# An eighth pair by plain products in the first block, and fewer dummy products in the lead, in a block-attention and feed-forward kernel

## The chip, the cores and the metric

The kernel runs on one core of one Trainium2 chip. The metric is the device time of one execution in microseconds (us), less is better. The five engines are named as in the profile: PE (TensorE, matrix products), DVE (VectorE), ACT (ScalarE), POOL (GpSimd) and SP (the engine whose queue issues most DMAs). PSUM is the memory into which PE writes, in eight banks; SBUF is the working memory.

## What is computed

Attention within chunks of 64 tokens, then a feed-forward layer with squared ReLU, all in float32:

```
q, k, v: (8 batches, 8 heads, 576 tokens, 64); 9 chunks of 64 tokens per batch and head
scores = q_c @ k_c.T / 8                 # per chunk and head
attn   = exp(scores - max) / (sum + 1e-9)
x      = (attn @ v_c), heads side by side    # 4608 tokens x 512
out    = (relu(x @ w_in) ** 2) @ w_out       # 512 -> 2048 -> 512
```

The weights `w_in` and `w_out` are float64 and reach the chip as two 32-bit words per element.

## The kernel before

**Pairs, units, blocks.** Two chunks are a pair (128 tokens, 36 pairs). Half of a pair's heads are a unit, so a pair has two. `blocks = [4] + [3] * 10 + [2]` (L63) groups the pairs into twelve blocks of 4, 3 and 2. For each block the feed-forward runs 16 steps (`NF`): step f multiplies x by 128 columns of `w_in` (`mm_in`, L603 to L612), ACT and DVE square the result and split it, and two steps later (`LAG`) `mm_out` (L647 to L656) adds its product with 128 rows of `w_out` to the block's output in PSUM. x, the squares and the weights are each held as a high and a low half in the format fp32r, and three products (high x high, high x low, low x high) stand for one. The last step of a block copies its outputs from PSUM (`store`, L658, copies on L663 and L665) and writes them out.

**Two ways through the attention.** The first `NN` pairs (seven: those of blocks 0 and 1) go by plain float32 products, class `Pair` (L472 to L581): PE turns q and k (L488), ACT copies them to `qbd` and `kt` (L497, L501), 16 score products (L509), DVE takes maximum, difference, sum and scaling (L517 to L535) with ACT's exponential between (L526), PE turns the probabilities (L547), ACT copies them (L552), 16 products with v (L561), and `place` writes x as high (ACT, L579) and low half (DVE, L581). All later pairs go by split halves, which cost PE less and DVE, ACT and POOL more: `s1` to `s4` and `norm` (L284 to L455), for one unit at a time. Their products are spread evenly among the feed-forward's products by `merge` (L682): while block b's steps run, the slots of block b + 1's units run beside them. Slot t holds the scores of unit t-1, the transposes of t-2 and the values of t-3, and so on (`attention_slot`, L585). Block 1 has twelve slots: one that opens the split path's tiles (`open_late`, L103), two empty ones (`HEAD`), and nine with attention (units 14 on, L923 to L927). Later blocks have six.

**The first block.** Block 0 also has to convert all 32 pieces of the weights (items) from float64 to two halves (`convert_w`, L142: two operations of ACT, four of DVE, then the high half on ACT, L182, and the low half on DVE, L191). Its order on all engines is written out by a planner (`Plan`, L697): operations are added with a cost, what they read and write, and a rank; at each step it takes the one that can start earliest, then the lowest rank. SP's operations are kept in the order in which they were added, so a load that waits for its room holds up all loads behind it. First comes the lead: four pairs with q, k and v from HBM, PE being given dummy bf16 products (`heat`, L779, 30 of them, and `warm_up`, L566, eight ahead of scores, turned probabilities and values of each of the four pairs). Pairs 4 to 6 follow among the conversions, added when the item number reaches 8, 14 and 20 (L889).

**Rooms.** Each item has a room of its own, `w0` to `w31`. Raw q and k of pair u lie in room `w31-u` until they are turned (L223), so the fetches of items 25 to 31 wait for that. v of a plain pair lies in `vbd0` or `vbd1`, by `pair % 2` (L99, L261); the load of pair 2's v waits until pair 0's products with v are done. Pairs outside the lead take all five PSUM tiles from the two banks named `at` (L805). x of blocks with even numbers shares one room, of odd ones another (`x_of`, L457).

Of the kernel before, what the change touches and what calls it, by code (L numbers as in the profile page):

```python
# [10 lines left out]
F32 = mybir.dt.float32  # L11
# [9 lines left out]
def kernel(  # L21
# [20 lines left out]
    nc = tc.nc  # L42
# [21 lines left out]
    LAG = 2  # L64
    HEAD = 2
    REST = 0
    GBUFS = 2
    RBUFS = 1

    WARM = 30  # L70
    WARM_P = 8
# [3 lines left out]

    NN = sum(blocks[:2])
    first_pair = [sum(blocks[:b]) for b in range(len(blocks))]
# [21 lines left out]
    qbd = [nat.tile([P, H, 2, CH], F32, name=f"qbd{n}") for n in range(2)]  # L99
    vbd = [nat.tile([P, H // 2, 2, 2, D], F32, name=f"vbd{n}") for n in range(2)]  # L100
    late = {}

    def open_late():  # L103
# [148 lines left out]
    def load_v(pair):  # L252


        if pair < NN:
            for c in range(2):
                bb, n0 = divmod(2 * pair + c, NCH)
                for h2, r in enumerate(halves):
                    s = v[bb, h2:H:2, n0 * CH:(n0 + 1) * CH, :]
                    nc.sync.dma_start(  # L260
                        out=vbd[pair % 2][r, :, c, h2, :], in_=s.rearrange("h i d -> i h d")  # L261
                    )
            return
        pairs[pair]["v"] = []
        for c in range(2):
            t = late["pool"].tile([P, H, D], F32, name=f"v_raw{pair}_{c}", tag="v_raw")
            pairs[pair]["v"].append(t)
            bb, n0 = divmod(2 * pair + c, NCH)
            s = v[bb, :, n0 * CH:(n0 + 1) * CH, :].rearrange("h i d -> i h d")
            for r in halves:  # L270
                nc.sync.dma_start(out=t[r], in_=s)
# [196 lines left out]
    def bank(which, shape, name):  # L468
        kind, n = which
        return psum[kind].tile(shape, F32, name=name, tag=f"{kind}{n}")  # L470

    class Pair:  # L472

# [21 lines left out]
        def keep_q(self, s):  # L495
            r = halves[s]
            nc.scalar.copy(qbd[self.u % 2][r, :, s], self.psq[r])  # L497

# [4 lines left out]
        def scores(self):  # L503


            self.sc = self.bank("sc", [P, H, CH])
            self.warm_up(self.sc.rearrange("p a b -> p (a b)"))
            for h in range(H):
                nc.tensor.matmul(  # L509
                    self.sc[:, h // 4 * 4 + h % 2 * 2 + h // 2 % 2],  # L510
                    qbd[self.u % 2][:, h].rearrange("p s i -> p (s i)"), self.kt[:, h],
                    start=True, stop=True,
                )
# [25 lines left out]
        def turn_p(self):  # L539


            ps = self.bank("pt", [P, HS // 2, 2, 2, CH])
            self.warm_up(ps.rearrange("p a b c d -> p (a b c d)"))
            e = self.e.rearrange("p (a c t) i -> p a c (t i)", t=2, c=2)
            for a in range(HS // 2):
                for c in range(2):
                    nc.tensor.transpose(ps[:, a, c].rearrange("p s i -> p (s i)"), e[:, a, c], ident)  # L547
            self.pt = ps
# [5 lines left out]
        def values(self):  # L554

            self.xt = self.bank("xt", [P, HH, 2, CH])
            self.warm_up(self.xt.rearrange("p a b c -> p (a b c)"))
            for hp in range(HH):
                s, a = divmod(hp, HS // 2)
                for c in range(2):  # L560
                    nc.tensor.matmul(  # L561
                        self.xt[:, hp, c], vbd[self.u % 2][:, hp, c].rearrange("p a d -> p (a d)"),
                        self.t[:, a, c, s], start=True, stop=True,
                    )

        def warm_up(self, ps):  # L566


            if self.lead:
                for _ in range(WARM_P):  # L570
                    nc.tensor.matmul(ps[:, :2 * P], warm_ops[:, :P], warm_ops, start=True, stop=True)

# [9 lines left out]

    warm_ops = ident.bitcast(mybir.dt.bfloat16)

# [11 lines left out]
    class Step:  # L596
# [6 lines left out]
        def mm_in(self, c, i):  # L603
            if c == 0 and i == 0:
                self.h = bank(("h", self.f % 2), [P, DM], f"h{self.b}_{self.f}")
            xh, xl = xt[self.b]
            wh, wl = wi[self.f]
# [160 lines left out]
    def first_block():  # L768


        p = Plan()
        add = p.add
        prs = [Pair(u) for u in range(NN)]

# [12 lines left out]
        def fetch(n):  # L787
            room = [("raw", n), ("q", n_items - 1 - n), ("k", n_items - 1 - n)]
            add(SP, ISSUE, lambda: fetch_w(n), writes=room, size=P * DM * 8)
# [6 lines left out]
        def load_values(u):  # L796
            add(SP, 4 * ISSUE, lambda: load_v(u), writes=[("v", u % 2)], size=P * DM * 4)

        def attention(u):
# [9 lines left out]
            for s in range(2):  # L809
                add(ACT, ONE, lambda s=s: x.keep_q(s), [bq], [("qbd", i, s)])  # L810
            add(PE, 4 * 0.11, lambda: x.turn(1), [("k", u), "ident"], [bk])
            add(ACT, ONE, x.keep_k, [bk], [("kt", i)])
            w = WARM_P * 0.11 if x.lead else 0
            add(PE, 16 * 0.11 + w, x.scores, [("qbd", i, 0), ("qbd", i, 1), ("kt", i)], [bs])
# [6 lines left out]
            add(ACT, ONE, x.keep_p, [bp], ["tt"])  # L821
            add(PE, 16 * 0.11 + w, x.values, [("v", i), "tt"], [bx])
            add(ACT, ONE, lambda: x.place(0), [bx], [("xh", u)])
            add(DVE, TWO, lambda: x.place(1), [bx, ("xh", u)], [("xl", u)])

# [37 lines left out]
        add(PE, WARM * 0.11, heat, ["ident"], [("at", 0)])  # L863
        for t in (qbd[0], vbd[0], qbd[1], vbd[1]):
            add(POOL, 0.95, lambda t=t: zero(t), [], [("qbd", i, s) for i in range(2) for s in range(2) if t is qbd[i]] + [("v", i) for i in range(2) if t is vbd[i]])
        lead = blocks[0]
        load(0)
        load_values(0)
        load(1)
        load_values(1)  # L870
        for u in range(2, lead):
            load(u)
        got = 2
        for n in range(got):
            fetch(n)
        for u in range(lead):
            p.rank = u
            attention(u)
            if u + 2 < lead:
                load_values(u + 2)  # L880
                fetch(got)
                got += 1
        for n in range(got):
# [3 lines left out]
        for n in range(got, n_items):  # L887
            p.rank = NN + n
            if u < NN and n >= 2 * got + 6 * (u - lead):  # L889
                load(u)  # L890
                load_values(u)
                attention(u)
                u += 1
            fetch(n)
            convert(n)
        add(SP, 16 * ISSUE, lambda: load_qk(NN), writes=["late"], size=2 * P * DM * 4)
        for f in range(NF):
# [4 lines left out]
            p.rank = -1  # L902
            square(f)
        p.run()

# [4 lines left out]
    with tc.manual_schedule(engines={PE}):  # L910
        for b in range(1, len(blocks)):
# [10 lines left out]
            if not last:  # L922
                n0 = NQ * first_pair[b + 1]  # L923
                n1 = n0 + NQ * blocks[b + 1]
                slots = [list(attention_slot(t, NQ * NN)) for t in range(n0 + 3 * (b > 1), n1 + 3)]
            if b == 1:
# [39 lines left out]
```

## Time and profile before

| what | us |
|---|---|
| median of 3 runs | 956.59 |
| lowest, highest | 955.41, 956.65 |
| the profiled execution | 956.33 |
| its span, first to last instruction | 954.2 |
| PE, DVE, ACT, POOL busy | 928.7, 708.5, 601.5, 216.8 |

The span is one profiled execution; the time is measured around it. In a line of the profile, `L609 PE MATMUL h<-xh,wi ... x1536 | 435.6, 340 | 3.0 <-DVE wi L191 1.6` is: line of the kernel, engine, operation, what is written from what, how many, busy time in us, mean duration of one in ns, and the engine's idle time ahead of them with what ended most of it. Products on PE are pipelined, so their durations overlap: the pace of PE is read from the distances between starts or from the chain of waits, not from the mean duration. A line of the timeline or of the chain begins with start and duration in us; `x12` means twelve instructions run together. A line of the windows has the stretch, its length, then busy time of PE, PE's weight loads (PEld), DVE, ACT and POOL, the granted TensorE clock as a share, the DMA share and GB/s.

### The profile page before, as it was taken

What the parts mean: (1) busy time and instruction counts of PE and PEld (TensorE: products, weight loads), DVE (VectorE), ACT (ScalarE), POOL (GpSimd) and SP (SyncE); (2) the same over time, 40 slices, a digit from 0 to 9 for tenths busy, and PEclk for the clock granted to TensorE, in tenths of its full rate; (3) what the DMA queues carried; (4) which work ended last, traced back from release to release, by engine and by line L of the source; (5) the groups of instructions that cost most, each with busy time, mean ns of one, the idle gap of its engine ahead of it and who ended that gap; (6) DMA issues with size and microseconds to landing.
All of it is one profiled execution on the core that took longest, in us unless ns stands there. A gap on an engine that the chain in (4) does not pass through costs nothing.

```text
span 954.2 us, 16935 instructions
## 1 busy us (share of the span) xinstructions
PE 928.7 (97%) x5046; PEld 828.8 (87%) x5046; DVE 708.5 (74%) x1634; ACT 601.5 (63%) x1491; POOL 216.8 (23%) x361
## 2 busy tenths in 40 slices
PE   9899999887999999999999999999999999999998
PEld 7788878766999999989999989989999999998997
DVE  3989995888777877777877877877878787753332
ACT  5688874677666766666766766666666666653232
POOL 1000002134222322333333323322222233311000
PEclk9999999999999999999999999999999999999999
DMA  6794505445533543433544544444444353210000
GB/s 161 192 295 136 177 1 117 85 92 105 111 74 75 111 77 71 104 74 74 111 78 78 111 79 75 94 93 78 77 109 81 72 113 62 56 40 9 4 34 23
DMA packets 292761, 86.06 MB, mean 90 GB/s; under 512 B 274112, under 2 KB 282304, under 8 KB 292672
## 3 DMA queue, kind: packets, MB, share of 16 engines
q1 hardware_dynamic: 290560, 84.47, 40.5%
q8 instruction: 41, 0.67, 0.3%
q10 hardware_dynamic: 2112, 0.52, 0.3%
q14 instruction: 48, 0.39, 0.1%
HBM read 52.69 MB, written 9.44 MB: 65 GB/s over the span
## 4 chain that ended last, share of the span: by engine, by line
PE 88%; DVE 5%; ACT 2%; DMA 2%; SPq 1%; issue 1%; POOL 0%; DVEq 0%; ACTq 0%; POOLq 0%
PE h L609 39%; PE o L653 38%; PE sc L346 3%; PE xt L430 3%; PE pt L396 1%; DMA woraw<-in_moe_w_out_dram 1%; PE sc L509 1%; SPq L250 1%; PE warm_ps L782 1%; PE xt L561 1%; ACT kst L305 0%; DMA k_raw<-in_k_dram 0%; DVE wi L191 0%; DVE wia L170 0%; ACT qst L299 0%
## 5 line engine op out<-in xcount | busy, mean ns | idle before, releaser
L609 PE MATMUL h<-xh,wi 128*128 128x384 f32 (+2 forms) x1536 | 435.6, 340 | 3.0 <-DVE wi L191 1.6
L653 PE MATMUL o<-wo,gh 128*128 128x512 f32 x1152 | 372.9, 397 | 0.0
L609 PEld LDWEIGHTS h<-xh,wi 128*128 128x128 f32 x1536 | 275.5, 189 | 18.4 <-DVE wi L191 3.1
L609 PE MATMUL h<-xl,wi 128*128 128x384 f32 (+2 forms) x768 | 261.1, 340 | 1.1 <-DVE xl L581 1.1
L653 PEld LDWEIGHTS o<-wo,gh 128*128 128x128 f32 x1152 | 208.5, 188 | 33.5 <-issue 0.2
L653 PE MATMUL o<-wo,gl 128*128 128x512 f32 x576 | 227.1, 394 | 0.0
L327 POOL TENSOR_TENSOR vs<-v_raw,vs 64x128 fp32r<-64x128 f32 x232 | 119.9, 517 | 250.1 <-ACT vs L324 234.3
L636 DVE TENSOR_TENSOR gl<-g,gh 128x384 fp32r<-128x384 f32 (+2 forms) x192 | 110.9, 578 | 64.5 <-ACT gh L633 60.9
L609 PEld LDWEIGHTS h<-xl,wi 128*128 128x128 f32 x768 | 145.0, 189 | 8.1 <-DVE xl L581 1.4
L624 DVE TENSOR_TENSOR g<-g 128x384 f32<-128x384 f32 (+1 forms) x176 | 99.2, 564 | 67.5 <-ACT g L620 65.7
L633 ACT CAST gh<-g 128x384 fp32r<-128x384 f32 (+2 forms) x192 | 98.5, 513 | 76.4 <-PE o L653 52.9
L620 ACT ACTIVATE g<-h 128x384 f32<-128x384 f32 (+2 forms) x192 | 94.5, 492 | 78.5 <-PE h L609 58.8
L653 PEld LDWEIGHTS o<-wo,gl 128*128 128x128 f32 x576 | 108.5, 188 | 20.5
L383 POOL TENSOR_TENSOR e<-e,z 128x256 f32<-128x256 f32 x58 | 46.0, 793 | 227.0 <-PE o L653 88.7
L358 DVE TENSOR_TENSOR e<-sc,e 64x128 f32<-64x128 f32 x232 | 67.0, 289 | 35.0 <-ACT e L356 30.3
L356 ACT COPY e<-sc 64x128 f32<-64x128 f32 x232 | 60.3, 260 | 47.4 <-PE sc L346 44.5
L444 DVE TENSOR_TENSOR x<-xt,x 64x128 f32<-64x128 f32 x232 | 67.0, 289 | 22.8 <-ACT x L442 17.5
L442 ACT COPY x<-xt 64x128 f32<-64x128 f32 x232 | 60.1, 259 | 35.8 <-PE xt L430 32.2
L346 PE MATMUL sc<-kst,qst 128*128 128x256 f32 x232 | 65.7, 283 | 5.5 <-DVE pst L414 3.3
L430 PE MATMUL xt<-pst,vs 128*128 128x256 f32 x232 | 65.2, 281 | 1.9 <-DMA pst<-pst 1.7
L450 POOL TENSOR_TENSOR xl<-x,xh 128x256 fp32r<-128x256 f32 x58 | 46.0, 793 | 61.0 <-ACT xh L449 58.7
L414 DVE TENSOR_TENSOR pst<-pt,pst 64x256 fp32r<-64x256 f32 x116 | 49.0, 422 | 11.7 <-ACT pst L410 7.7
(78 smaller groups left out, 909.3 us busy)
## 6 DMA issues: line engine op xcount, KB each, us to landing
v_raw<-in_v_dram SPq DMA_DIRECT2D x116, 128.0 KB, 3.3
out_dram<-ob SPq DMA_DIRECT2D x36, 256.0 KB, 2.1
wiraw<-in_moe_w_in_dram SPq DMA_DIRECT2D x16, 512.0 KB, 6.4
woraw<-in_moe_w_out_dram SPq DMA_DIRECT2D x16, 512.0 KB, 6.2
q_raw<-in_q_dram SPq DMA_DIRECT2D x232, 32.0 KB, 2.0
k_raw<-in_k_dram SPq DMA_DIRECT2D x232, 32.0 KB, 2.1
qst<-ql SPq DMA_DIRECT2D x58, 128.0 KB, 2.6
kst<-kst SPq DMA_DIRECT2D x58, 128.0 KB, 2.6
```

Source lines behind the costliest of these rows:

```text
L327: nc.gpsimd.tensor_tensor(vs[:, c][dst], vr[dst], vs.bitcast(F32)[:, c][dst], op=ALU.subtract)
L346: nc.tensor.matmul(ps.rearrange("p w c j -> p (w c j)"), late["q"][:, hh].rearrange("p c i -> p (c i)"), late["k"][:, :, :, hh], start=Tru ...
L356: nc.scalar.copy(e[r], ps[r, :, 1, c])
L358: nc.vector.tensor_tensor(e[r], ps[r, :, 0, c], e[r], op=ALU.add)
L430: nc.tensor.matmul(st["xt"][hp][:, c].rearrange("p w a q -> p (w a q)"), st["v"][:, c, hp].rearrange("p a d -> p (a d)"), late["p"][:, :, ...
L444: nc.vector.tensor_tensor(x[r, hp], ps[hp][r, :, 0, h2], x[r, hp], op=ALU.add)
L609: nc.tensor.matmul(self.h[:, :self.n], a[:, c], bb[:, c, :self.n], start=c == 0 and i == 0, stop=c == NCC - 1 and i == 2,)
L620: nc.scalar.activation(self.g, self.h[:, :self.n], AF.Relu)
L624: nc.vector.tensor_tensor(self.g, self.g, self.g, op=ALU.mult)
L633: nc.scalar.copy(self.gh[:, :self.n], self.g)
L636: nc.vector.tensor_tensor(self.gl[:, :self.n], self.g, self.gh.bitcast(F32)[:, :self.n], op=ALU.subtract)
L653: nc.tensor.matmul(acc[b, j], a[:, j * P:(j + 1) * P], bb, start=f == 0 and i == 0, stop=f == NF - 1 and i == 2,)
```

## The change

Five things change.

- `NN` becomes 8: the first pair of block 2 also goes by plain products, in block 0's stretch. Its x belongs to block 2, whose room is that of block 0's x, so its `place` is added after the last step of block 0. In the order of attention outside the lead, pairs now follow every four items (8, 12, 16, 20). Block 1's slots begin at unit 16: seven instead of nine.
- `HEAD` becomes 1: one empty slot instead of two. Block 1 has nine slots in all.
- Dummy products: 18 instead of 30 at the start; eight ahead of each of three stages for the first and the last pair of the lead only; and eight more ahead of the first product of the feed-forward.
- v of pairs 2 and 3 gets rooms of its own, in `w22` and `w21`, whose items are fetched after these pairs' values. With that the loads of the lead are put in another order: q and k of three pairs ahead of the first v, and the fetches of four items among the rest.
- The second half of q's copy moves from ACT to DVE for pairs 0 and 1.

```diff
--- before.py
+++ after.py
@@ -62,18 +62,19 @@
     PRIO = 300
     blocks = [4] + [3] * 10 + [2]
     LAG = 2
-    HEAD = 2
+    HEAD = 1
     REST = 0
     GBUFS = 2
     RBUFS = 1
 
-    WARM = 30
+    WARM = 18
     WARM_P = 8
     assert sum(blocks) == NPAIR
     MAXB = max(blocks)
     XB = (max(blocks[::2]), max(blocks[1::2]))
 
-    NN = sum(blocks[:2])
+
+    NN = sum(blocks[:2]) + 1
     first_pair = [sum(blocks[:b]) for b in range(len(blocks))]
 
     const = ctx.enter_context(tc.tile_pool(name="const", bufs=1))
@@ -98,7 +99,13 @@
     nat = early.enter_context(tc.tile_pool(name="nat", bufs=1))
     qbd = [nat.tile([P, H, 2, CH], F32, name=f"qbd{n}") for n in range(2)]
     vbd = [nat.tile([P, H // 2, 2, 2, D], F32, name=f"vbd{n}") for n in range(2)]
+
+    for n in range(2, blocks[0]):
+        vbd.append(const.tile([P, H // 2, 2, 2, D], F32, name=f"vbd{n}", tag=f"w{2 * DFF // P - NN - n}"))
     late = {}
+
+    def slot_of(pair):
+        return pair if pair < blocks[0] else pair % 2
 
     def open_late():
 
@@ -258,7 +265,7 @@
                 for h2, r in enumerate(halves):
                     s = v[bb, h2:H:2, n0 * CH:(n0 + 1) * CH, :]
                     nc.sync.dma_start(
-                        out=vbd[pair % 2][r, :, c, h2, :], in_=s.rearrange("h i d -> i h d")
+                        out=vbd[slot_of(pair)][r, :, c, h2, :], in_=s.rearrange("h i d -> i h d")
                     )
             return
         pairs[pair]["v"] = []
@@ -469,6 +476,14 @@
         kind, n = which
         return psum[kind].tile(shape, F32, name=name, tag=f"{kind}{n}")
 
+    warm_ops = ident.bitcast(mybir.dt.bfloat16)
+
+    def warm_up(ps):
+
+
+        for _ in range(WARM_P):
+            nc.tensor.matmul(ps[:, :2 * P], warm_ops[:, :P], warm_ops, start=True, stop=True)
+
     class Pair:
 
 
@@ -494,7 +509,9 @@
 
         def keep_q(self, s):
             r = halves[s]
-            nc.scalar.copy(qbd[self.u % 2][r, :, s], self.psq[r])
+
+            copy = nc.vector.tensor_copy if s and self.u < 2 else nc.scalar.copy
+            copy(qbd[self.u % 2][r, :, s], self.psq[r])
 
         def keep_k(self):
             self.kt = nat.tile([P, H, CH], F32, name=f"kt{self.u}", tag=f"kt{self.u % 2}")
@@ -504,7 +521,8 @@
 
 
             self.sc = self.bank("sc", [P, H, CH])
-            self.warm_up(self.sc.rearrange("p a b -> p (a b)"))
+            if self.u in (0, blocks[0] - 1):
+                warm_up(self.sc.rearrange("p a b -> p (a b)"))
             for h in range(H):
                 nc.tensor.matmul(
                     self.sc[:, h // 4 * 4 + h % 2 * 2 + h // 2 % 2],
@@ -540,7 +558,8 @@
 
 
             ps = self.bank("pt", [P, HS // 2, 2, 2, CH])
-            self.warm_up(ps.rearrange("p a b c d -> p (a b c d)"))
+            if self.u in (0, blocks[0] - 1):
+                warm_up(ps.rearrange("p a b c d -> p (a b c d)"))
             e = self.e.rearrange("p (a c t) i -> p a c (t i)", t=2, c=2)
             for a in range(HS // 2):
                 for c in range(2):
@@ -554,21 +573,15 @@
         def values(self):
 
             self.xt = self.bank("xt", [P, HH, 2, CH])
-            self.warm_up(self.xt.rearrange("p a b c -> p (a b c)"))
+            if self.u in (0, blocks[0] - 1):
+                warm_up(self.xt.rearrange("p a b c -> p (a b c)"))
             for hp in range(HH):
                 s, a = divmod(hp, HS // 2)
                 for c in range(2):
                     nc.tensor.matmul(
-                        self.xt[:, hp, c], vbd[self.u % 2][:, hp, c].rearrange("p a d -> p (a d)"),
+                        self.xt[:, hp, c], vbd[slot_of(self.u)][:, hp, c].rearrange("p a d -> p (a d)"),
                         self.t[:, a, c, s], start=True, stop=True,
                     )
-
-        def warm_up(self, ps):
-
-
-            if self.lead:
-                for _ in range(WARM_P):
-                    nc.tensor.matmul(ps[:, :2 * P], warm_ops[:, :P], warm_ops, start=True, stop=True)
 
         def place(self, part):
             b = block_of[self.u]
@@ -580,7 +593,6 @@
             else:
                 nc.vector.tensor_tensor(xl, ps, xh.bitcast(F32), op=ALU.subtract)
 
-    warm_ops = ident.bitcast(mybir.dt.bfloat16)
 
     def attention_slot(t, lo=0, hi=NU):
 
@@ -603,6 +615,8 @@
         def mm_in(self, c, i):
             if c == 0 and i == 0:
                 self.h = bank(("h", self.f % 2), [P, DM], f"h{self.b}_{self.f}")
+                if self.b == 0 and self.f == 0:
+                    warm_up(self.h)
             xh, xl = xt[self.b]
             wh, wl = wi[self.f]
             a, bb = ((wh, xh), (wh, xl), (wl, xh))[i]
@@ -769,6 +783,7 @@
 
 
         p = Plan()
+        lead = blocks[0]
         add = p.add
         prs = [Pair(u) for u in range(NN)]
 
@@ -785,7 +800,10 @@
             nc.gpsimd.memset(t, 0.0)
 
         def fetch(n):
-            room = [("raw", n), ("q", n_items - 1 - n), ("k", n_items - 1 - n)]
+            m = n_items - 1 - n
+            room = [("raw", n), ("q", m), ("k", m)]
+            if 2 <= m + 1 - NN < lead:
+                room.append(("v", m + 1 - NN))
             add(SP, ISSUE, lambda: fetch_w(n), writes=room, size=P * DM * 8)
 
         def load(u):
@@ -794,7 +812,7 @@
                 add(e, 2 * ISSUE, lambda n=n: load_one(u, n), writes=[("qk"[n], u)], size=P * DM * 4)
 
         def load_values(u):
-            add(SP, 4 * ISSUE, lambda: load_v(u), writes=[("v", u % 2)], size=P * DM * 4)
+            add(SP, 4 * ISSUE, lambda: load_v(u), writes=[("v", slot_of(u))], size=P * DM * 4)
 
         def attention(u):
             x = prs[u]
@@ -807,10 +825,11 @@
             x.banks = {"q": bq, "k": bk, "sc": bs, "pt": bp, "xt": bx}
             add(PE, 4 * 0.11, lambda: x.turn(0), [("q", u), "ident"], [bq])
             for s in range(2):
-                add(ACT, ONE, lambda s=s: x.keep_q(s), [bq], [("qbd", i, s)])
+                e = DVE if s and u < 2 else ACT
+                add(e, ONE, lambda s=s: x.keep_q(s), [bq], [("qbd", i, s)])
             add(PE, 4 * 0.11, lambda: x.turn(1), [("k", u), "ident"], [bk])
             add(ACT, ONE, x.keep_k, [bk], [("kt", i)])
-            w = WARM_P * 0.11 if x.lead else 0
+            w = WARM_P * 0.11 if u in (0, lead - 1) else 0
             add(PE, 16 * 0.11 + w, x.scores, [("qbd", i, 0), ("qbd", i, 1), ("kt", i)], [bs])
             add(DVE, TWO, x.top, [bs], [("m", i)])
             add(DVE, TWO, x.less, [bs, ("m", i)], [("e", i)])
@@ -819,9 +838,16 @@
             add(DVE, TWO, x.norm, [("z", i)], [("e", i)])
             add(PE, 4 * 0.11 + w, x.turn_p, [("e", i), "ident"], [bp])
             add(ACT, ONE, x.keep_p, [bp], ["tt"])
-            add(PE, 16 * 0.11 + w, x.values, [("v", i), "tt"], [bx])
-            add(ACT, ONE, lambda: x.place(0), [bx], [("xh", u)])
-            add(DVE, TWO, lambda: x.place(1), [bx, ("xh", u)], [("xl", u)])
+            add(PE, 16 * 0.11 + w, x.values, [("v", slot_of(u)), "tt"], [bx])
+            if u < NN - 1:
+                place(u)
+
+        def place(u):
+            x = prs[u]
+            j = u if u < NN - 1 else 0
+            bx = x.banks["xt"]
+            add(ACT, ONE, lambda: x.place(0), [bx], [("xh", j)])
+            add(DVE, TWO, lambda: x.place(1), [bx, ("xh", j)], [("xl", j)])
 
         def convert(n):
             words, clamp, shift, sign, up, high, low = convert_w(n)
@@ -861,32 +887,29 @@
 
         add(POOL, 0.4, prepare, [], ["ident"])
         add(PE, WARM * 0.11, heat, ["ident"], [("at", 0)])
-        for t in (qbd[0], vbd[0], qbd[1], vbd[1]):
-            add(POOL, 0.95, lambda t=t: zero(t), [], [("qbd", i, s) for i in range(2) for s in range(2) if t is qbd[i]] + [("v", i) for i in range(2) if t is vbd[i]])
-        lead = blocks[0]
-        load(0)
-        load_values(0)
-        load(1)
-        load_values(1)
-        for u in range(2, lead):
+        for i in range(lead):
+            if i < 2:
+                add(POOL, 0.95, lambda i=i: zero(qbd[i]), [], [("qbd", i, 0), ("qbd", i, 1)])
+            add(POOL, 0.95, lambda i=i: zero(vbd[i]), [], [("v", i)])
+        for u in range(lead):
             load(u)
-        got = 2
+            if u > 1:
+                load_values(u - 2)
+        got = lead
         for n in range(got):
             fetch(n)
+            if n + 2 < lead:
+                load_values(n + 2)
         for u in range(lead):
             p.rank = u
             attention(u)
-            if u + 2 < lead:
-                load_values(u + 2)
-                fetch(got)
-                got += 1
         for n in range(got):
             p.rank = NN + n
             convert(n)
         u = lead
         for n in range(got, n_items):
             p.rank = NN + n
-            if u < NN and n >= 2 * got + 6 * (u - lead):
+            if u < NN and n >= 2 * got + 4 * (u - lead):
                 load(u)
                 load_values(u)
                 attention(u)
@@ -901,6 +924,7 @@
                 ffn_out(f - LAG)
             p.rank = -1
             square(f)
+        place(NN - 1)
         p.run()
 
     with tc.manual_schedule(engines={PE, DVE, ACT, SP, POOL}):
@@ -920,9 +944,9 @@
                     ops.append(s.act)
             slots = [[]]
             if not last:
-                n0 = NQ * first_pair[b + 1]
-                n1 = n0 + NQ * blocks[b + 1]
-                slots = [list(attention_slot(t, NQ * NN)) for t in range(n0 + 3 * (b > 1), n1 + 3)]
+                n0 = NQ * first_pair[b + 1] + 3 if b > 1 else NQ * NN
+                n1 = NQ * (first_pair[b + 1] + blocks[b + 1])
+                slots = [list(attention_slot(t, NQ * NN)) for t in range(n0, n1 + 3)]
             if b == 1:
                 slots = [[open_late]] + [[] for _ in range(HEAD)] + slots
 
```

## The prediction

> **What bounds the kernel now.** I read the page's head, then the first copies of outputs on ScalarE, to get the length of each block, then the windows over those blocks, then what TensorE waits for, and last the lead (the first 43 us) instruction by instruction.
>
> ```profile
> span 954.2 us, 16935 instructions
> PE 928.7 (97%) x5046; PEld 828.8 (87%) x5046; DVE 708.5 (74%) x1634; ACT 601.5 (63%) x1491; POOL 216.8 (23%) x361
> ```
>
> The profiled execution took 956.33 us, 2.1 us more than its span; the median of the runs is 956.59. I sum against 956.3. TensorE looks full at 97%, but that is an average. The first output copy of each block comes at the same place in each block's order of products, so its start times give the lengths (timeline of ScalarE):
>
> ```profile
> 153.46 0.58 ACT L665 COPY ob<-o 128x512 f32<-128x512 f32 x1
> ...
> 247.63 0.59 ACT L665 COPY ob<-o 128x512 f32<-128x512 f32 x1
> ...
> 321.38 0.59 ACT L665 COPY ob<-o 128x512 f32<-128x512 f32 x1
> ```
>
> From block 0's mark to block 1's is 94.2 us, from block 1's to block 2's 73.75, with nearly the same products: 20.4 us too much. The windows between those marks (busy time of each engine) and, in the same view, the lead and one later stretch:
>
> ```profile
> 12.00:43.30 31.30, 26.99 (x238) 24.74 (x236) 26.78 (x52) 20.99 (x37) 0.00 (x0) 1.00 0.72 195
> ...
> 43.30:50.00 6.70, 6.64 (x26) 5.38 (x27) 6.49 (x13) 5.01 (x10) 0.00 (x0) 0.75 0.72 194
> 50.00:60.00 10.00, 10.00 (x54) 8.55 (x53) 5.87 (x10) 8.93 (x16) 0.00 (x0) 1.00 0.90 280
> ...
> 153.50:247.60 94.10, 81.74 (x420) 70.25 (x419) 75.31 (x185) 58.98 (x159) 26.19 (x45) 0.98 0.53 103
> 247.60:321.40 73.80, 73.80 (x398) 67.05 (x397) 58.48 (x143) 48.98 (x132) 21.88 (x37) 1.00 0.44 88
> ```
>
> Block 2's stretch has no idle TensorE. Block 1's has 12.4 us without even a modelled matmul, and VectorE (third pair, 75.31) works much harder. What TensorE waits for there (waits, 174 to 247.6 us):
>
> ```profile
> PE pt L396 <- DVE x L444: 6.3, 3, 2.3
> ```
>
> The transposes of the probabilities stand behind VectorE. So block 1 isn't bound by products but by the attention squeezed into it, and the rest of the kernel, from block 2 on, by products.
>
> **The change in block 1.** Prices per part, from block 2's own rows:
>
> ```profile
> 257.44 2.09 PE h L609 x12
> ...
> 282.73 2.08 PE o L653 x9
> ```
> ```profile
> L636 DVE TENSOR_TENSOR gl<-g,gh 128x384 fp32r<-128x384 f32 x16 | 9.3, 581 | 4.0 <-ACT gh L633 3.8
> L624 DVE TENSOR_TENSOR g<-g 128x384 f32<-128x384 f32 x16 | 9.1, 568 | 3.3 <-ACT g L620 3.0
> ```
>
> A step of the feed-forward takes 2.09 + 2.08 = 4.17 us of TensorE, 16 steps 66.7; the remaining 7.0 of 73.75 are six units (half pairs), 1.17 each. VectorE's 58.48 us hold 18.4 for the steps (1.15 each), so 40.1 for six units, 6.7 each.
>
> Before, block 1 has 12 slots (one opens the late tiles, two are empty, nine hold attention), 16/12 = 1.33 steps each. A slot with one unit in each stage needs 1.33 x 4.17 + 1.17 = 6.7 us of TensorE but 6.7 + 1.33 x 1.15 = 8.2 of VectorE. Nine slots x 1.5 = 13.5 us of stall at least. Of the 20.4, some 1.8 are work: the run-up holds scores of eight units, transposes of seven and values of six where block 2 has six of each (about 0.4 a stage, 1.2), and block 0's last step has four pairs instead of three (0.6). So 18.6 us are stall: 13.5 by throughput, some 5 from queues that stand in order.
>
> After, there are 9 slots (one, one, seven), 1.78 steps each: TensorE 1.78 x 4.17 + 1.17 = 8.6 us, VectorE 6.7 + 2.04 = 8.7. The throughput part falls to 7 x 0.1, under 1; the other, scaled by slots (7/9 of 5), to 4. I take 5 us. Bounds: 0, as block 2 shows at 9.8 us of VectorE in slots of 12.3; and 11, if VectorE gets no further than 85% (it was at 75.31 of 94.10, 80%): 8.7/0.85 - 8.6 = 1.6, seven times. Work falls as well: scores of six units, transposes of five, values of four are 1.2 below block 2. So 73.75 + 0.6 - 1.2 + 5 = 78.2 instead of 94.2: **-16.0 us** (-10 to -21).
>
> **The eighth pair in block 0.** Its parts at TensorE's full pace (chain of waits, in order of time):
>
> ```profile
> 1.37 6.20 PE warm_ps L782 x30
> ...
> 17.16 0.44 PE q L488 x4
> ...
> 19.34 1.73 PE xt L561 x16
> 21.08 0.87 PE pt L571 x8
> ...
> 23.26 1.75 PE sc L509 x16
> ...
> 43.35 4.07 PE h L609 x11
> ...
> 82.74 2.72 PE o L653 x12
> ```
>
> Three sets of turns (0.44 each), scores 1.75 and values 1.73 are 4.8 us, on an engine that from 43.35 to block 0's end has hardly a gap: all of it counts, **+4.8**. (The two units it replaces cost 2.3, and that is in block 1's sum.) VectorE's share:
>
> ```profile
> L521 DVE TENSOR_TENSOR ne<-sc,nm 128x512 f32<-128x512 f32 x7 | 4.8, 691 | 0.2
> ...
> L532 DVE RECIPROCAL nz<-nz 128x8 f32<-128x8 f32 x7 | 1.4, 203 | 0.2
> ...
> L531 DVE TENSOR_SCALAR nz<-nz 128x8 f32<-128x8 f32 x7 | 1.2, 172 | 0.2
> ```
>
> Four full passes (maximum, difference, sum, scaling, all taken at 691 ns) and two small ones: 3.1 us; the two half copies of q that move from ScalarE to VectorE, bounded by the same 691 ns, add up to 1.4 in the lead. VectorE had 4.1 us idle from 50 to 60 us, because its weights came late: the queue held them back.
>
> ```profile
> 20.88 2.61 SPq L260 DMA_DIRECT2D vbd<-in_v_dram x4
> ...
> 45.27 0.60 SPq L139 DMA_DIRECT2D woraw<-in_moe_w_out_dram x1
> ...
> 95.42 0.37 SPq L137 DMA_DIRECT2D wiraw<-in_moe_w_in_dram x1
> ```
> ```profile
> 35.42 0.66 ACT L152 ACTIVATE wia<-wiraw 128x512 f32<-128x512 f32 x1 [2.07 <-DMA wiraw<-in_moe_w_in_dram]
> ```
>
> With own rooms for pairs 2 and 3 the loads of v no longer wait for values of pairs 0 and 1, so the fetches behind them go out up to 10 us sooner. That cover is what pays VectorE's 4.5; without it block 0 would end about 4 us later. The copy of x into the first block's room comes after block 0's last input product, on ScalarE and VectorE, one pass each, beside block 1's first products; the PSUM bank that it frees isn't needed until the two slots without attention are over (2 x 1.78 x 4.17 = 15 us): nothing.
>
> **The lead.** q and k of pair 0 are there well before the 30 dummies end:
>
> ```profile
> L234 ACTq DMA_DIRECT2D qk_raw<-in_k_dram x2: 436/496/557, 1.4 to 1.8; - x2
> ...
> DMA to landing us min/median/max: 2.4/3.4/3.6
> ```
>
> k lands by 1.8 + 3.6 = 5.4, the dummies end at 7.58. Eighteen end at 1.37 + 18 x 0.207 = 5.1, so the first turn starts 2.2 us sooner, and pair 1's q, now issued ahead of v, is ready too. Of the rest, six groups of dummies at 0.87 (5.2 us) and ScalarE's 2.07 us stall go, but VectorE is busy 26.78 of the lead's 31.3 us and gets two copies more, so at most 31.3 - 28.1 = 3.2 can be won. I take half: the first step starts 2.2 + 1.6 = **3.8 us** sooner (2.2 to 5.4; 0 if something else was late).
>
> The first 11 products took 4.07 us; at 2.72/12 they need 2.5, and the granted clock there was 0.75. Eight dummies now stand ahead of them, while TensorE waits for x anyway. I count half of 1.6, **-0.8** (0 to -1.6).
>
> Here a rule speaks against the change. The 30 dummies ran at 207 ns each, the later groups of eight at 109. The Trainium skill's page "TensorE: Matmul & The Clock Gate" (Part 1) says why: TensorE is throttled to half rate by default, a window of about 3.4 us of activity frees it, one of idleness throttles it again. No run here shows yet what 18 dummies do; by an estimate from its figure, 18 x 0.207 = 3.7 us of them are hardly more than one window.
>
> **The weights' gate.** Fetches into the raw rooms of q and k wait until a pair has been turned: before, seven wait for pair 6, after, eight for pair 7.
>
> ```profile
> 72.11 0.60 PE L488 MATMUL k<-ident,qk_raw 128*128 128x128 f32 x4
> ...
> 94.79 0.60 PE L488 MATMUL k<-ident,qk_raw 128*128 128x128 f32 x4
> ```
> ```profile
> wiraw<-in_moe_w_in_dram SPq DMA_DIRECT2D x16, 512.0 KB, 6.4
> ```
> ```profile
> L191 DVE TENSOR_TENSOR wi<-wia,wi x12: 681/684/693, 26.4 to 113.4; 128x512 fp32r<-128x512 f32 x12
> L191 DVE TENSOR_TENSOR wo<-woa,wo x10: 681/684/685, 38.1 to 110.0; 128x512 fp32r<-128x512 f32 x10
> ```
>
> Pairs 4 to 7 share two PSUM banks and so go one after another, 22.7 us apart. Pair 4's k was turned about 72.1 - 22.7 = 49.4; three pairs later is 117.5, or 113.7 if the lead's 3.8 carries over, and the first of the eight lands 6.4 later, at 120 to 124. VectorE has 22 of 32 weights done by 117 and needs the 25th at about 119. That is 1 to 5 us late, with pair 7's own work to fill in: **+1**.
>
> **Sum.** Block 0: 4.8 - 3.8 - 0.8 + 1 = +1.2. Block 1: -16.0. From block 2 on the slots are the same. 956.3 + 1.2 - 16.0 = **941.5 us**.
>
> **Rivals.**
> 1. *The stalls stay as they are per slot* (order of queues and hops, not VectorE's load): 18.6 x 7/9 = 14.5 left, so block 1 takes 87.7, and 956.3 + 1.2 - 6.5 = 951. For it: VectorE was at 80%, not full. Against: block 2, with the same order in longer slots, has none. Chance 0.10.
> 2. *The clock falls in the lead*: pairs 1 and 2 run at half rate, 2 x 4.8 us more on TensorE, less 5.2 of dummies gone, so the lead is about 4.4 longer than forecast and the first products as cold as before: 941.5 + 4.4 + 0.8 = 947. The 0.75 after gaps of a microsecond speaks for it; that TensorE was busy 27.0 of 31.3 us, and still has 19 us of real work there, against. Chance 0.06. This is how the named page's rule would act.
> 3. *The lead hides nothing*: dummies and rooms weren't what it waited for, so the first step starts when it did: 941.5 + 3.8 = 945. The 2.2 us of dummies after k's landing speak against. Chance 0.07.
> 4. *Slower: the weights' gate.* If a fourth pair and denser ranks (every four weights instead of six) stretch a pair's passage from 22.7 to 29 us, pair 7's k is turned at 49.4 + 3 x 29 = 136.4, the first weight lands at 142.8, 23.8 us after VectorE needs it, and all products of the last steps stand behind: 956.3 + 0.2 + 23.8 - 16.0 = 964. It turns the sign from a passage of about 27 us. Against: VectorE stays as busy as it was, and ranks only order what is ready. Chance 0.05.
> 5. *Nothing changes* on balance (block 0 loses what block 1 wins): 956. Chance 0.02.
>
> **How the numbers follow.** The forecast has 0.70. Its own range takes block 1's -10 to -21 and block 0's ends (-2.2 without the gate, +6 with no shorter lead): 931 to 950 without adding all bad ends up; it also holds rivals 2 and 3. About 0.8 is inside. A measurement of this kernel can tell 0.2%, 1.9 us. Faster: 0.70 + 0.10 + 0.06 + 0.07, less a little for their tails, 0.91; within 0.2% 0.03; slower 0.06.
>
> **What would show it.** Right: first copies of block 0 and 1 some 78 us apart, at about 155 and 233; block 2 at 73.75 as before; TensorE's waits on VectorE in block 1 under 5 us; first turn near 5.1, first step near 39.5; pair 7's k turned near 114. Wrong: copies 85 us or more apart (rival 1); 207 ns products after 10 us in the lead (rival 2); a first step at 43 (rival 3); VectorE idle before a weight's landing after 110 us (rival 4).

## The result and the profile after

The changed kernel takes 939.11 us (937.73 to 940.98) against 956.60: a ratio of 0.982 (95% interval 0.980 to 0.984), 17.5 us less. The forecast was 941.5. The profiled execution took 938.83 us. Head of the page of the changed kernel:

```profile
span 937.1 us, 16737 instructions
PE 920.8 (98%) x5018; PEld 824.8 (88%) x5018; DVE 698.9 (75%) x1607; ACT 592.2 (63%) x1463; POOL 212.6 (23%) x351
```

The first output copies of blocks 0, 1 and 2 (timeline of ScalarE; the copy is now line 679):

```profile
149.60 0.58 ACT L679 COPY ob<-o 128x512 f32<-128x512 f32 x1
...
230.24 0.59 ACT L679 COPY ob<-o 128x512 f32<-128x512 f32 x1
...
304.84 0.59 ACT L679 COPY ob<-o 128x512 f32<-128x512 f32 x1
```

Block 0 ends 3.9 us sooner (149.60 for 153.46), block 1 takes 80.6 us for 94.2, a gain of 13.5, and block 2's mark comes 74.6 after, where it was 73.75. With half a microsecond over the rest of the span that makes its 17.1. So the total was nearly as forecast, but from other shares: +1.2 and -16.0 were said, -3.9 and -13.5 came. Block 0 came out 5.1 us better and block 1 2.5 us worse; that the two errors had opposite signs is luck.

In the windows between the marks (PE first, VectorE third; they stop 1.2 and 2.0 us ahead of the marks), block 1's idle TensorE shrinks from 12.4 to 5.3 us, and block 2 looks as before:

```profile
149.70:229.00 79.30, 73.98 (x388) 64.82 (x387) 59.32 (x145) 46.28 (x123) 18.74 (x31) 1.00 0.49 96
229.00:302.80 73.80, 73.31 (x394) 66.04 (x393) 57.75 (x138) 48.43 (x129) 21.45 (x36) 1.00 0.44 88
```

What TensorE still waits for there (waits, 140 to 235 us; total, times, longest), and below it the three waits of the kernel before that stood beside the 6.3 us of the transposes:

```profile
PE pt L403 <- DVE x L451: 2.1, 2, 1.3
PE xt L437 <- DMA pst<-pst: 1.2, 1, 1.2
PE sc L353 <- DVE pst L421: 0.9, 2, 0.5
PE sc L353 <- DMA kst<-kst: 0.7, 1, 0.7
```
```profile
PE sc L346 <- DVE pst L414: 3.3, 5, 1.0
PE sc L346 <- DMA kst<-kst: 2.2, 1, 2.2
PE xt L430 <- DMA pst<-pst: 0.5, 1, 0.5
```

The wait of the transposes on VectorE fell from 6.3 to 2.1 us and the two of the scores from 5.5 to 1.6; the wait of the values for a DMA grew from 0.5 to 1.2. The lead (timeline of TensorE):

```profile
1.38 3.81 PE L797 MATMUL warm_ps<-ident 128*128 128x256 bf16 x18 [1.38 <-POOL ident masks.py:199]
5.03 0.60 PE L503 MATMUL q<-ident,qk_raw 128*128 128x128 f32 x4
...
26.78 1.97 PE L581 MATMUL xt<-tt,vbd 128*128 128x64 f32 x16 [1.74 <-ACT ne L544]
28.58 1.75 PE L485 MATMUL pt<-ident 128*128 128x256 bf16 x8
...
30.98 1.61 PE L485 MATMUL xt<-ident 128*128 128x256 bf16 x8
...
36.10 0.50 PE L623 MATMUL h<-xl,wi 128*128 128x512 f32 x1 [0.60 <-DVE xl L594]
```

The first turn starts at 5.03 (5.1 was said), the first step gets its low half of x at 36.10 instead of 43.35. The eight dummies at 28.58 took 1.75 us and those at 30.98 took 1.61, where every group of eight took 1.03 or 1.04 in the kernel before: here the clock fell.

### The profile page after: what moved, and what is told of

The parts are those of the page before. It is cut to its first block, busy times and chain, and to the rows that moved or that the text cites. A ratio compares the mean times of both kernels' runs of the same rounds, so it can differ in the third digit from the quotient of the medians.

```text
span 937.1 us, 16737 instructions
## 1 busy us (share of the span) xinstructions
PE 920.8 (98%) x5018; PEld 824.8 (88%) x5018; DVE 698.9 (75%) x1607; ACT 592.2 (63%) x1463; POOL 212.6 (23%) x351
## 4 chain that ended last, share of the span: by engine, by line
PE 86%; DVE 5%; DMA 4%; ACT 2%; issue 1%; SPq 1%; POOL 1%; DVEq 0%; POOLq 0%; ACTq 0%
PE h L623 39%; PE o L667 38%; PE xt L437 3%; PE sc L353 3%; PE pt L403 1%; DMA wiraw<-in_moe_w_in_dram 1%; DMA q_raw<-in_q_dram 1%; DMA pst<-pst 1%; PE xt L581 1%; PE sc L527 1%; DMA kst<-kst 1%; DMA v_raw<-in_v_dram 0%; SPq L267 0%; POOL vbd L800 0%; DVE wia L177 0%
## 5 line engine op out<-in xcount | busy, mean ns | idle before, releaser
L334 POOL TENSOR_TENSOR vs<-v_raw,vs 64x128 fp32r<-64x128 f32 x224 | 116.2, 519 | 241.6 <-ACT vs L331 227.8
L365 DVE TENSOR_TENSOR e<-sc,e 64x128 f32<-64x128 f32 x224 | 64.7, 289 | 34.1 <-ACT e L363 29.4
L363 ACT COPY e<-sc 64x128 f32<-64x128 f32 x224 | 58.2, 260 | 42.2 <-PE sc L353 39.0
L451 DVE TENSOR_TENSOR x<-xt,x 64x128 f32<-64x128 f32 x224 | 64.7, 289 | 23.4 <-ACT x L449 19.3
L449 ACT COPY x<-xt 64x128 f32<-64x128 f32 x224 | 58.0, 259 | 36.5 <-PE xt L437 33.1
L437 PE MATMUL xt<-pst,vs 128*128 128x256 f32 x224 | 62.7, 280 | 2.7 <-DMA pst<-pst 2.6
L353 PE MATMUL sc<-kst,qst 128*128 128x256 f32 x224 | 62.9, 281 | 2.2 <-DVE pst L421 1.4
```

The source lines that it names most:

```text
L334: nc.gpsimd.tensor_tensor(vs[:, c][dst], vr[dst], vs.bitcast(F32)[:, c][dst], op=ALU.subtract)
L353: nc.tensor.matmul(ps.rearrange("p w c j -> p (w c j)"), late["q"][:, hh].rearrange("p c i -> p (c i)"), late["k"][:, :, :, hh], start=Tru ...
L363: nc.scalar.copy(e[r], ps[r, :, 1, c])
L365: nc.vector.tensor_tensor(e[r], ps[r, :, 0, c], e[r], op=ALU.add)
L437: nc.tensor.matmul(st["xt"][hp][:, c].rearrange("p w a q -> p (w a q)"), st["v"][:, c, hp].rearrange("p a d -> p (a d)"), late["p"][:, :, ...
L451: nc.vector.tensor_tensor(x[r, hp], ps[hp][r, :, 0, h2], x[r, hp], op=ALU.add)
```

## The experiments

Every kernel was run beside the kernel before on the same chip. The kernel before took 956.26 to 957.37 us there, so a difference between the medians of two rows is good to about 1 us, and the ratios are the safer comparison. Times in us; the first step is the start of the first product with xl, the mark the first copy of block 0, and block 1's length is from mark to mark, all from one profile each. Four of the kernels have the same block 1 (the changed kernel, e1, e11 and e12); it took 80.4 to 81.0 us in them, which is the noise of that column.

| kernel | median | ratio to before, 95% interval | first step | mark | block 1 |
|---|---|---|---|---|---|
| before | 956.6 | | 43.35 | 153.46 | 94.2 |
| after | 939.11 | 0.980 to 0.984 | 36.10 | 149.60 | 80.6 |
| e1 pair only | 944.19 | 0.985 to 0.989 | 42.52 | 155.87 | 80.4 |
| e2 lead only | 952.38 | 0.994 to 0.997 | 38.01 | 147.94 | 94.9 |
| e3 two empty slots | 941.92 | 0.983 to 0.986 | 37.93 | 149.94 | 84.2 |
| e4 squares on ScalarE | 938.52 | 0.979 to 0.983 | 36.69 | 149.17 | 80.2 |
| e5 no squares | 939.09 | 0.981 to 0.984 | 37.83 | 151.69 | 79.5 |
| e6 extra VectorE pass | 941.91 | 0.984 to 0.987 | 37.30 | 151.05 | 81.8 |
| e7 no empty slot | 943.05 | 0.985 to 0.988 | 38.98 | 152.31 | 83.6 |
| e8 squares on GpSimd | 938.52 | 0.981 to 0.984 | 38.41 | 151.94 | 79.7 |
| e9 third bank | 938.76 | 0.980 to 0.982 | 38.14 | 151.88 | 79.3 |
| e10 third bank, before | 955.96 | 0.998 to 1.000 | 43.15 | 154.90 | 93.7 |
| e11 all dummies | 944.36 | 0.986 to 0.989 | 46.14 | 155.80 | 81.0 |
| e12 v loads in shared rooms | 946.45 | 0.988 to 0.990 | 48.46 | 157.54 | 81.0 |

The first step came between 36.1 and 39.0 in the nine profiles with the changed lead (the changed kernel and e2 to e9), so the 36.10 is the earliest of them and the middle one is 37.9.

**e1 and e2: the two halves alone.**

```diff
 e1, on the kernel before
-    HEAD = 2
+    HEAD = 1
-    NN = sum(blocks[:2])
+    NN = sum(blocks[:2]) + 1
...
+        place(NN - 1)
...
 e2, on the changed kernel: the same lines undone
```

> The kernel before with the eighth pair, its late place, the ranks of every four items and the nine slots of block 1 alone; dummies, rooms of v, load order and copies as before. My theory (block 1's stall falls with its attention, the pair costs block 0 its 4.8 us of TensorE): block 1 takes 80.6 us between marks as in the changed kernel instead of 94.2, block 0's mark comes about 5 us later than before, 948 us in all. Rival (the pair's 4.8 us hide in gaps of block 0): block 0's mark where it was, 943. Rival (without earlier weights VectorE's extra work delays block 0 as well): 952.

> The changed kernel with seven plain pairs and the old twelve slots: fewer dummies, own rooms, load order and copies stay. Theory (what the first step wins is kept to the end of block 0): first step 7 us sooner, block 0's mark 7 us sooner, block 1 still 94 us, 949.5 in all. Rival (VectorE's conversions set the end of block 0, so the lead's gain is waited away): first step sooner, mark at most 2 us sooner, 954 or more.

The marks of e1, and then of e2:

```profile
155.87 0.58 ACT L665 COPY ob<-o 128x512 f32<-128x512 f32 x1
...
236.23 0.59 ACT L665 COPY ob<-o 128x512 f32<-128x512 f32 x1
```
```profile
147.94 0.58 ACT L679 COPY ob<-o 128x512 f32<-128x512 f32 x1
...
242.88 0.59 ACT L679 COPY ob<-o 128x512 f32<-128x512 f32 x1
```

e1 has all of block 1's gain (80.4), as its theory said, but pays only 2.4 us in block 0 instead of 5, so its 944.19 lies nearer the first rival's 943 than the theory's 948. e2 has none of block 1's gain (94.9) and ends block 0 5.5 us sooner, as much as its first step came sooner (5.3). That is its theory in kind, with less than the 7 us that were expected; its 952.38 lies between the theory's 949.5 and the rival's 954. The medians, 12.1 and 3.9 less than their kernel before, make 16.0 of the 17.5, so the halves are nearly independent. From first step to mark e1 takes 113.35 us, the changed kernel 113.5, the kernel before 110.1 and e2 109.9: the pair costs 3.2 to 3.6 there, not 4.8. What hid the rest fits the waits on weights: the kernel before waits 1.9 us for `wi` in block 0 (the two lines below), e2 2.0, e1 not at all and the changed kernel 0.2.

```profile
PE h L609 <- DVE wi L191: 1.6, 3, 0.7
...
PE h L609 <- ACT wi L182: 0.3, 1, 0.3
```

**e3 and e7: the length of block 1's slots.**

```diff
 e3
-    HEAD = 1
+    HEAD = 2
 e7
-    HEAD = 1
+    HEAD = 0
```

> The changed kernel with two empty slots in block 1 instead of one: ten slots of 1.6 steps, the same attention. Theory (VectorE's load per slot sets the stall): TensorE needs 7.8 us a slot, VectorE 8.5, so seven slots x 0.7 instead of 0.1 stall, 4 us more in block 1, 943. Rival (the order of the queues costs so much a slot, whatever the slot's length): the stall is the same, 939.

> The changed kernel with no empty slot in block 1: eight slots of two steps. Theory (VectorE's load per slot): TensorE 2 x 4.17 + 1.17 = 9.5, VectorE (6.7 + 2.3)/0.91 = 9.9, 0.4 x 7 = 2.8 of stall, block 1 at 76 us, 934.5. Rival (order and hops per slot): 80.6, 939. Rival (the split path's tiles and v now come too late for the first slot): 942.

e3 gave 3.6 us more in block 1 and 2.8 in the median, the size that the first theory asked for; e5 and e6 below take its reason away. e7's longer slots gave 2.9 us more, not 4.6 less: its third theory. TensorE's waits in e7, 150 to 236 us:

```profile
PE sc L353 <- DMA kst<-kst: 5.4, 2, 4.8
PE pt L403 <- DVE x L451: 0.9, 1, 0.9
PE xt L437 <- DMA pst<-pst: 0.3, 1, 0.3
```

4.8 us are one wait of the first scores for their stacked k; without an empty slot the split path starts before its data is ready. The granted clock was 0.96 over that stretch, for 1.00 in the changed kernel. The other waits are shorter than in the changed kernel.

**e4, e5, e6, e8: is it VectorE's load?**

```diff
 e4: if self.b > 1 instead of if self.b, so that block 1 squares on ScalarE
 e5: if self.b == 1, no square at all
 e6: before the low half
+            if self.b == 1:
+                nc.vector.tensor_tensor(self.gl[:, :self.n], self.g, self.g, op=ALU.mult)
 e8: if self.b == 1
+                nc.gpsimd.tensor_tensor(self.g, self.g, self.g, op=ALU.mult)
```

> The changed kernel with block 1's squares on ScalarE instead of VectorE. Theory (VectorE's load per slot): VectorE loses 1.8 x 0.57 = 1.0 us of 8.7 a slot, block 1's stall of some 7.5 us falls to 4 or less, 935.5. Rival (order of the queues, ScalarE's work stands ahead of attention copies): no gain or a loss, 939 to 941.

> The changed kernel with block 1's squares left out (its outputs are those of relu(x w_in) w_out), so VectorE loses 1.0 us a slot and no engine gains any. Moving them to ScalarE did nothing, perhaps because ScalarE became as full. Theory (VectorE's load per slot; in the changed kernel, with two empty slots and before, slots took its load over 0.91): 7.7/0.91 = 8.5 us, less than TensorE's 8.6, so block 1's 80.6 us fall to 76 or less, 934.5 in all. Rival (order and hops cost some 1.1 us a slot whatever the load): 80 us, 938 to 939.

> The changed kernel with one more VectorE pass per step of block 1 (a product written to the low half before the real one), 1.0 us a slot. Theory (VectorE's load per slot): 9.7/0.91 = 10.7 us a slot, 2.1 x 7 = 14.6 of stall, block 1 at 88 us, 946. Rival (order and hops): 82 us at most, 940.

> The changed kernel with block 1's squares on GpSimd, which has room. Theory (VectorE's load per slot): as without squares, block 1 at 76 us, 934.5. Rival (GpSimd takes some 1.2 us for a square, by 792 ns for 256 columns, and its queue holds the attention's own work up): 80 us or more, 939 to 942.

Marks of e5, then of e6:

```profile
151.69 0.58 ACT L681 COPY ob<-o 128x512 f32<-128x512 f32 x1
...
231.23 0.59 ACT L681 COPY ob<-o 128x512 f32<-128x512 f32 x1
```
```profile
151.05 0.58 ACT L681 COPY ob<-o 128x512 f32<-128x512 f32 x1
...
232.80 0.59 ACT L681 COPY ob<-o 128x512 f32<-128x512 f32 x1
```

One VectorE pass per step less or more moved block 1 by 1.1 us each way, 79.5 and 81.8. That is about twice the noise of the column, and e6's granted clock was 0.98 over the block for 1.00, so its 1.1 may be the clock's. The theory of VectorE's load asked for 4.6 less and 7 more; it fell. e4 and e8 (80.2, 79.7) agree: with nine slots the rest of the stall isn't VectorE's throughput. For the twelve slots of the kernel before this was not tried.

**e9 and e10: is it the PSUM banks?** All of TensorE's waits on VectorE in block 1 above are for a bank to be emptied: the split path turns five tiles a slot over two banks. In the cut below, `spare[0]` is true while block 1's steps are issued.

```diff
+    def at_bank():
+        n = next(turn_at)
+        if not spare[0]:
+            return ("at", n % 2)
+        return (("at", 0), ("at", 1), ("o", 3))[n % 3]
```

> The changed kernel with a third PSUM bank for the split path while block 1's steps run: the output bank of the fourth pair, which no block uses then. VectorE's load did not set the stall: with the squares left out or a pass added, block 1 moved by 1.1 us where 6 to 7 were expected. Theory (five uses a slot turn over two banks, so a transpose waits until VectorE has emptied the bank of the values before it): TensorE's waits on VectorE go, block 1's 80.6 us fall to 77 or less, 935.5 or less. Rival (the waits are those of the attention's own chain of engines and move to DMA or to the probabilities): 80, 938 to 939.

> The kernel before with the same third bank in block 1, twelve slots, eight units. Theory (bank turnover): most of the 18.6 us of stall go, block 1's 94.2 fall to 83 or less, 945. Rival (VectorE's throughput, as the prediction had it, at least 13.5 of the 18.6): 89 or more, 951 or more.

e9's waits, 150 to 230 us, largest first:

```profile
PE xt L445 <- DVE g L646: 1.4, 1, 1.4
PE sc L361 <- ACT xh L464: 1.4, 1, 1.4
PE sc L361 <- DMA kst<-kst: 0.7, 1, 0.7
PE xt L445 <- DMA pst<-pst: 0.7, 1, 0.7
```

The transposes no longer wait, but scores and values do, and block 1 won 1.3 us where 3.6 were asked for. The theory of the banks fell too; the rival, that the waits move, held. In the kernel before the bank won 0.5 us of 18.6, and VectorE's throughput, which the prediction put at 13.5 of them, wasn't contradicted there.

**e11 and e12: what shortened the lead.**

```diff
 e11: WARM = 30, and warm_up under if self.lead in scores, turn_p and values
 e12
     def slot_of(pair):
-        return pair if pair < blocks[0] else pair % 2
+        return pair % 2
```

> The changed kernel with the old dummy products back: 30 at the start and eight ahead of three stages of all four pairs. The granted clock stays at 1.00 up to the first step, where the changed kernel has 0.5 to 0.8 from 30 to 35 us. Theory (dummies stood on the way to the first step): the first turn 2.2 us later, the first step at about 40 instead of 36.1 to 39.0, 941.5. Rival (rooms and load order made the lead shorter, and the clock that is kept pays for the dummies): first step at 38 or sooner, 939.

> The changed kernel with pairs 2 and 3 loading v into the rooms of pairs 0 and 1 again, in the changed order of loads. Theory (own rooms let the fetches behind go out early, which pays VectorE's extra work): weights 3 to 33 come about 5 us later, the first step 2 us later, VectorE idle between 45 and 60 us, 942. Rival (conversions have slack): 939.

e11's first step came at 46.14, 10.0 us later than in the changed kernel and later than before the change, and some 5 us were lost in all (5.3 between the medians). Both theories were wrong. The dummies that came back hardly stood on the way themselves: the first turn came at 6.16, 1.1 us later. What stood on the way was VectorE, busy with hardly a gap from 20.3 us on. Ahead of the last low half of x it made 28 passes of weight conversion in e11, 18 in the changed kernel and 23 in the kernel before. A weight takes five (0.42, 0.43, 0.69, 0.69 and 0.68 us, 2.9 together), and the ten passes more are 5.8 of the 7.0 us by which that low half came later. The other 3.0 are TensorE's, which turns pair 4's k and runs the eight last dummies only then. The planner orders by its own estimates, and dummies count in them; that this is why more conversions went ahead is the likely reading, but no run shows it alone. Part of the loss comes back, since e11 goes from first step to mark in 109.7 us for 113.5.

Nor was the clock kept. It stayed at 1.00 up to 40 us (PE's clock is the third figure from the end) and was 0.70 from 40 to 45, around a wait for VectorE just ahead of the first step. Windows and timeline of e11, and below them the windows of the changed kernel:

```profile
30.00:35.00 5.00, 3.24 (x31) 2.93 (x29) 4.79 (x12) 2.96 (x6) 0.00 (x0) 1.00 1.11 260
...
40.00:45.00 5.00, 2.63 (x16) 2.08 (x16) 4.86 (x10) 4.79 (x10) 0.00 (x0) 0.70 0.98 336
```
```profile
43.09 1.11 PE L503 MATMUL k<-ident,qk_raw 128*128 128x128 f32 x4 [2.37 <-DVE xl L594]
44.00 1.91 PE L485 MATMUL h<-ident 128*128 128x256 bf16 x8
```
```profile
25.00:30.00 5.00, 3.26 (x25) 2.85 (x25) 4.86 (x12) 4.07 (x8) 0.00 (x0) 0.87 1.04 379
30.00:35.00 5.00, 5.00 (x38) 4.43 (x36) 4.86 (x10) 3.55 (x6) 0.00 (x0) 0.78 0.93 197
```

e12 missed its aim. In the changed order the loads of pairs 2 and 3 are added ahead of the first products with v, so sharing rooms made pairs 0 and 1 use the v of pairs 2 and 3 and come after those loads, rather than make the later loads wait. Pair 0's products with v start at 20.64 instead of 17.86. Its loss of some 7 us has other parts as well: six weights were done ahead of its first step (48.46), as in e11, and the clock was 0.50 from 30 to 45 us. So it doesn't show what the own rooms bring; that part was not tried by itself, nor was q's copy on VectorE.

## Why the prediction was right, and where its terms were off

**Block 1, -16.0: came as -13.5.** Right in what it rested on: the excess of 20.4 us stood in block 1, came from attention squeezed into it, and went with fewer units in longer slots (e1 has it all, e2 none). Wrong in the division of the stall. The step that failed is "Nine slots x 1.5 = 13.5 us of stall at least", carried over as "The throughput part falls to 7 x 0.1": it counts VectorE as full in each slot and takes the rest for small. With nine slots nothing was left of throughput by that step, and 80.6 - 73.2 = 7.4 us of stall stayed (73.2 is block 1's work by the prediction's sum; TensorE's idle time is 5.3) where 5 were said; e5 and e6 show that VectorE's load moves it by 1.1 us at most. What moves it is the slot's length: the same seven slots stall 11.0 us in all in e3, where they are shorter, and 7.4 in the changed kernel. Stall per slot, by TensorE's own work in a slot, each worked out as the prediction does: 2.1 us at 6.7 (before), 1.6 at 7.8 (e3), 1.1 at 8.6 (after), at most 0.8 at 9.5 (e7 without its first wait: (83.6 - 73.2 - 4.8)/7), none at 12.3 (block 2). Two of these hold some lower clock: 0.96 over block 1 in e7, at most 3.3 us of its 5.6, and 0.98 in the kernel before (0.83 from 230 to 240 us, at most 1.7 of its 18.6). In the kernel before, how much of the 2.1 a slot is VectorE's throughput stays open. The chain of waits of the changed kernel at one such place, where the values wait 1.2 us:

```profile
198.92 0.52 ACT gh L647
199.46 0.26 ACT e L363
199.73 0.27 ACT e L363
200.00 0.13 SPq L419
...
200.23 3.78 DMA pst<-pst
...
204.14 0.36 PE xt L437
```

A square's half and a copy of scores on ScalarE, the issue on SP, a DMA that takes 3.8 us to land, then the values on TensorE. With work taken off VectorE (e4, e5, e8) the same kinds of waits stayed, and with a bank more (e9) others came in their place; no run shortened a link on ScalarE, on SP or in the DMA. That it is the chain as a whole is the reading that fits all of them. It is argued, not shown, and which link would pay most stays open.

**The pair, +4.8: came as 3.2 to 3.6.** The duration fits, "all of it counts" was not right: some 2 us of waits for weights lay in the same stretch.

**The lead, -3.8 and -0.8: came as -7.25** in this profile, -5.4 in the middle one of the nine. The step that failed is the half taken between "at most 3.2 can be won" and nothing, under a bound that counted conversions of weights done ahead as fixed. They aren't: four were done before, three after, and e11 shows six; at 2.9 us of VectorE each, one weight less lifts the bound of 5.4 us in all to 8.3. The first products gained more than the 0.8 that was said: eight now take 2.12 us at one stretch (0.27 each; eleven took 4.07 before), so eleven would gain 1.2. That the last dummies did it isn't shown. The clock was full again when they began at 34.17, since all eight took 1.04, and in e11 the same eight took 1.91 and products behind them 0.63 each.

**The gate, +1: did not show.** Pair 7's k was turned at 103, not at 114 (pairs 5, 6 and 7):

```profile
67.90 0.60 PE L503 MATMUL k<-ident,qk_raw 128*128 128x128 f32 x4
...
85.14 0.60 PE L503 MATMUL k<-ident,qk_raw 128*128 128x128 f32 x4
...
103.05 0.60 PE L503 MATMUL k<-ident,qk_raw 128*128 128x128 f32 x4
```

A pair passes in 17 to 18 us, not 22.7, so the rival that turned the sign at 27 was far off.

**The rivals.** The first (stall per slot whatever the load) named the mechanism better than the forecast did, but not the price: it scaled the stall of 6.7 us slots by their number, and longer slots have less each. The second came in part: the clock fell to 0.78 between 30 and 35 us, on no longer gap than 1.74. The Trainium skill's "TensorE: Matmul & The Clock Gate" (Part 1) asks for a window of about 3.4 us without activity; the length of the gap here doesn't agree with that. The sign that the prediction named did show, 219 ns for each dummy at 28.58, but with pair 3 and not with pairs 1 and 2. The fall cost the two groups of dummies at 28.58 and 30.98 some 1.3 us together, on a lead that still came out shorter. In other profiles of the same lead it cost more: pair 2's products with v took 3.65 us in e8 for 1.97 here, and over the nine the first step tends to come later where the clock from 30 to 35 us is lower (36.10 at 0.78, 36.69 at 0.73, 38.98 at 0.50). The third (the lead hides nothing) is ruled out by e2, the fifth (no change on balance) by the result.

No variant beats the changed kernel beyond the intervals: e4, e8 and e9 lie 0.4 to 0.6 us below it.

## What to carry to other kernels

When work is spread evenly beside a stream of products, look at the time per slot before the load per engine: attention that costs nothing in slots of 12.3 us stalled TensorE 1.1 us a slot at 8.6 and 2.1 at 6.7, and taking load off one engine won 1 us of 7. Work moved out of the crowded stretch is worth its stall, not its own time: here the pair cost 3.2 to 3.6 us in block 0, and block 1, which also lost an empty slot, won 13.5. And a planner that orders by estimated times reorders everything when a cost is added: the 60 dummies that e11 put back delayed the first turn by 1.1 us and the first step by 10.0, of which 5.8 were conversions that VectorE now made ahead of it.

## What the runs showed of the hardware

The granted clock fell to 0.78 over 30 to 35 us, with TensorE busy 6.3 of the 8 us before and no gap above 1.74 us in the changed kernel's profile; it fell to between 0.50 and 0.73 in the eight other profiles of the same lead, behind one gap of 1.83 to 2.41 us. In e11 a gap of 1.76 us at 33 us left it at 1.00 from 35 to 40, and one of 2.37 at 43 came with 0.70 over 40 to 45. Moving the square in block 1 to GpSimd cost nothing in all (e8, 938.52), though GpSimd's busy time from 150 to 231 us was 31.5 us, where the changed kernel has 18.8 to 230 us.
